# Block attention and an MLP on one core: inputs ahead of the layer-2 weights, and sixteen tiles transposed by the DMA crossbar

## The chip, the core and the metric

The kernel runs on one core of a Trainium2 chip. A core has five engines with instruction queues of their own: PE (matrix products and transposes, results in PSUM), DVE, ACT and POOL (elementwise work) and SP, which here only issues DMAs. The DMAs that SP issues form one hardware queue (q1 in the profile), those that POOL issues form another, software-driven one (q0). The metric is the device time in microseconds; the kernel before was timed three times, with a median of 247.38 us (247.32 to 247.84).

## What is computed

The inputs q, k and v have the shape (4, 8, 768, 64): batch, heads, positions, head dimension. The reference, cut to what matters:

```python
for b in range(nb):                                    # blocks of 64 positions
    intra = einsum(einsum(qb, kb) * Dmask, vb)         # decaying causal mask
    inter = einsum(qb * lam_pow, kv_state)
    out[:, :, sl] = intra + inter
    kv_state = lam_block * kv_state + einsum(kb * rev_pow, vb)
x  = out with the heads side by side                   # (4, 768, 512)
xn = (x - mean) / sqrt(var + 1e-06) * g_ln
y  = x + maximum(xn @ w_ch1, 0) @ w_ch2                # 512 -> 2048 -> 512
```

## The kernel before

**Tiles.** The 3072 rows (4 batches of 768) are 24 tiles of 128 rows, numbered t. Each tile passes through five steps, and then through the MLP in a group of one to four tiles.

- `p0(t)` (line 289) issues the loads of tile t+4 (`load_tile`, three DMAs of 256 KB on SP: kin, qin, vin) and turns tile t's inputs into bf16 on POOL (`bf_inputs`: kb line 142, qb line 144, vb line 146).
- `p1(t)` transposes kb and qb on PE (tk line 153, tq line 162); ACT copies tk to kTp and DVE copies tq to qT (ACT for the first four tiles).
- `p2(t)` multiplies kb by vb (pk, line 177), updates the state (Stmp on DVE line 184, Sn on POOL line 185), and makes the scores (sc, line 192), which DVE masks into mA (line 194).
- `p3(t)` makes the attention output po (lines 203 and 207), copies it to x on ACT (line 210) and lets DVE form the statistics and the centred, scaled bf16 tile xc (line 216).
- `p4(t)` transposes xc by four PE matmuls against an identity (xt, line 230), copies the result to the group's tile xT on ACT (line 231), and forms 1/std (lines 233 and 235).

`mlp(g)` gives two kinds of units. `m1(u)` multiplies xT by layer-1 weights (pm, line 254), with a ReLU on ACT into hT (line 257). `m2(i, part)` is four matmuls of hT by layer-2 weights (pm, line 267); after the fourth part DVE forms the output tile o (line 278) and SP stores it (line 280).

**Weights.** The weights are loaded by POOL in four chunks each, with a cast from float32 (w_0 to w_3 of layer 1 at line 75, of layer 2 at line 78). A chunk is 1 MB in HBM and 512 KB in the core's memory.

**Order.** All queues run in the order of the program text. Lines 309 to 353 are a hand-written start: four tiles of attention with the loading of weights between, the MLP of groups 0 and 1 (tiles 0 to 3), whose m2 units run chunk by chunk over three of the four tiles, and the attention of tiles 4 to 7 placed between MLP units by the table `after`. In it `load_tile(4, after_pool=True)` (line 319) puts a tiny memset into tile 4's input buffer on POOL, so that SP starts this load only when POOL has come there; tile 5 has the same at line 322. From line 356 on, a planner interleaves the steps of tiles 8 to 23 with the units of groups 4 to 9: after each unit it runs as many steps as a pace asks for, and all steps up to a group's last p4 within the last units before that group starts. The group sizes are 2, 2, 1, 1, 2, 3, 3, 4, 4, 2.

**Waits.** Each DMA of SP also waits for the DMA eight places earlier on that queue, since eight semaphores go round. The input buffers hold six tiles.

Of the kernel before, what the change touches and what calls it, by code (L numbers as in the profile page):

```python
# [8 lines left out]
BF16 = mybir.dt.bfloat16  # L9
# [7 lines left out]
def kernel(  # L17
# [30 lines left out]
    wk = ctx.enter_context(tc.tile_pool(name="wk", bufs=3))  # L48
    xp = ctx.enter_context(tc.tile_pool(name="xp", bufs=11))
    gp = ctx.enter_context(tc.tile_pool(name="gp", bufs=2))  # L50
    ps = ctx.enter_context(tc.tile_pool(name="ps", bufs=1, space=PSUM))


    qkv_in = {}

    def load_tile(t, after_pool=False):
        b, c = divmod(t, nb)
        got = {}
        for name, src in (("k", k), ("q", q), ("v", v)):
# [5 lines left out]
            nc.sync.dma_start(f, src[b, :, c * C:(c + 1) * C, :].rearrange("h p d -> p h d"))  # L65
            got[name] = f
        qkv_in[t] = got
# [6 lines left out]
    def load_w1(c):  # L74
        nc.gpsimd.dma_start(w1[c], moe_w_ch1[:, c * W1C:(c + 1) * W1C].rearrange("(k p) f -> p k f", p=128))
# [14 lines left out]
    ident = const.tile([128, 128], BF16)  # L90
# [19 lines left out]
    lamC = const.tile([128, NP, 128], F32)  # L110
# [17 lines left out]
    lam_cp = lam_c.rearrange("p (a two) -> p a two", two=2)  # L128
    nc.vector.tensor_copy(lamC[0:64, :, 0:64], lam_cp[0:64, :, 0:1].to_broadcast([64, NP, 64]))
    nc.vector.tensor_copy(lamC[64:128, :, 64:128], lam_cp[64:128, :, 1:2].to_broadcast([64, NP, 64]))  # L130


    st = {}
# [2 lines left out]
    mv_keep = {}  # L136
    xT_of = {}

    def bf_inputs(t):
        f = qkv_in.pop(t)  # L140
        kb = wk.tile([128, H, D], BF16, tag="kb", bufs=4, name="kb")
        nc.gpsimd.tensor_copy(kb, f["k"])  # L142
        qb = wk.tile([128, H, D], BF16, tag="qb", name="qb")
        nc.gpsimd.tensor_tensor(qb, f["q"], lam_q[:, :, None].to_broadcast([128, H, D]), op=ALU.mult)  # L144
        vb = wk.tile([128, H, D], BF16, tag="vb", bufs=4, name="vb")
        nc.gpsimd.tensor_tensor(vb, f["v"], lam_v[:, :, None].to_broadcast([128, H, D]), op=ALU.mult)  # L146
        st[t] = dict(qb=qb, kb=kb, vb=vb)

    def p1(t):
        s = st[t]  # L150
# [47 lines left out]
    def p3(t):  # L198
        s = st[t]
        po = ps.tile([128, H, D], F32, tag="po", bufs=1, name="po")  # L200
        inter = s["S"] is not None
        for h in range(H):
            nc.tensor.matmul(po[:, h, :], lhsT=s["mA"][:, h, :], rhs=s["vb"][:, h, :],  # L203
                             start=(h == 0), stop=(not inter and h == H - 1), skip_group_check=True)
        if inter:
            for p in range(NP):
                nc.tensor.matmul(po[:, 2 * p:2 * p + 2, :], lhsT=s["qT"][:, p, :], rhs=s["S"][:, p, :],  # L207
                                 start=False, stop=(p == NP - 1), skip_group_check=True)
        x = xp.tile([128, DM], F32, tag="x", name="x")
        nc.scalar.copy(x, po.rearrange("p h d -> p (h d)"))  # L210
        stats = wk.tile([128, 6], F32, tag="stats", name="stats")
        nc.vector.bn_stats(stats, x)  # L212
        mv = xp.tile([128, 2], F32, tag="mv", name="mv")
        nc.vector.bn_aggr(mv, stats)
        xc = wk.tile([128, DM], BF16, tag="xc", name="xc")
        nc.vector.scalar_tensor_tensor(xc, in0=x, scalar=mv[:, 0:1], in1=g_row, op0=ALU.subtract, op1=ALU.mult)  # L216
        s["xc"], s["mv"], s["x"] = xc, mv, x

    def p4(t):
        s = st.pop(t)  # L220
        g = group_of[t]
# [3 lines left out]
        if t < 2:  # L225
            xt = ps.tile([128, KA, 128], BF16, tag="mm", bufs=3, name="xt")
        else:
            xt = ps.tile([128, KA, 128], BF16, tag="aux", bufs=2, name="xt")
        for kk in range(KA):
            nc.tensor.transpose(xt[:, kk, :], s["xc"][:, kk * 128:(kk + 1) * 128], ident)  # L230
        nc.scalar.copy(xT_of[g][:, :, i * 128:(i + 1) * 128], xt)  # L231
# [49 lines left out]

        return m1, m2

    sizes = [2, 2, 1, 1, 2, 3, 3, 4, 4, 2]
    groups = [list(range(sum(sizes[:i]), sum(sizes[:i + 1]))) for i in range(len(sizes))]
    assert groups[-1][-1] == NT - 1
    group_of = {t: g for g, ts in enumerate(groups) for t in ts}

    def p0(t):
        if t > 3 and t + 4 < NT:  # L290
            load_tile(t + 4)
        bf_inputs(t)


    def p3_p0(t):
        p3(t)
        if t + 3 < NT:
            p0(t + 3)

    def round_of(j):  # L300
        steps = [(p1, j), (p3_p0, j - 1), (p2, j), (p4, j - 2)]
        return [(f, t) for f, t in steps if t < NT]

    def run(*steps):
        for f, *a in steps:
            f(*a)


    p0(0)
    p0(1)  # L310
    run((p1, 0), (p2, 0), (p0, 2), (p1, 1), (p3, 0), (p2, 1))
    load_w1(0)
    load_w1(1)
    run((p1, 2), (p3, 1))
    p0(3)
    load_w1(2)
    run((p2, 2), (p4, 0), (p1, 3), (p3, 2), (p2, 3), (p4, 1))
    load_w1(3)
    load_tile(4, after_pool=True)
    for c in range(NWC):  # L320
        load_w2(c)
    load_tile(5, after_pool=True)
# [5 lines left out]
    def m1s(f, c):  # L328
        for u in range(c * m1a.count // NWC, (c + 1) * m1a.count // NWC):
            f(u)  # L330

    m1s(m1a, 0)
    run((p3, 3), (p4, 2))
    m1s(m1a, 1)
    p4(3)
    m1s(m1a, 2)
    p0(4)
    for c in range(3):
        m1s(m1b, c)
    m1s(m1a, 3)  # L340
# [14 lines left out]

    steps = []
    for j in range(8, NT + 2):
        steps += [s for s in round_of(j) if s not in ((p3_p0, 7), (p4, 7), (p4, 6))]
# [12 lines left out]
    for u, (f, *a) in enumerate(plan):  # L371
        f(*a)

        rate = max([(upto(g) - pace) / max(1, at - 2 - u) for g, at in starts.items() if at > u] + [0.0])
        pace = min(len(steps), pace + rate)
        due = max([upto(g) for g, at in starts.items() if u < at <= u + 3] + [int(pace + 1e-6)])
        run(*steps[pos:due])
        pos = max(pos, due)
    run(*steps[pos:])
# [29 lines left out]
```

## Time and profile before

| | |
|---|---|
| median of three timed runs | 247.38 us |
| the profiled execution's own time | 246.76 us |
| its span, first to last instruction | 245.0 us |
| PE busy | 219.0 us (89%) |
| ACT, DVE, POOL busy | 121.1, 112.9, 92.9 us |
| HBM read, written | 27.53 MB, 6.29 MB |
| DMA, by queue | q1 25.43 MB in 78624 packets, q0 4.19 MB in 4224 packets |

Busy time is the union of an engine's instructions; the ends of matmuls are modelled and neighbours overlap, so that four short matmuls of 0.22 us each in the chain of work show 0.39 us in the timeline. In a timeline a row gives the start, the duration, the engine, the line, the operation, out<-in, the count, and in brackets the idle time of the engine before it with what ended it. The chain of work follows the work that ended last back from the end. The granted clock (PEclk) is the share of full speed that TensorE was given.

### The profile page before, as it was taken

What the parts mean: (1) busy time and instruction counts of PE and PEld (TensorE: products, weight loads), DVE (VectorE), ACT (ScalarE), POOL (GpSimd) and SP (SyncE); (2) the same over time, 40 slices, a digit from 0 to 9 for tenths busy, and PEclk for the clock granted to TensorE, in tenths of its full rate; (3) what the DMA queues carried; (4) which work ended last, traced back from release to release, by engine and by line L of the source; (5) the groups of instructions that cost most, each with busy time, mean ns of one, the idle gap of its engine ahead of it and who ended that gap; (6) DMA issues with size and microseconds to landing.
All of it is one profiled execution on the core that took longest, in us unless ns stands there. A gap on an engine that the chain in (4) does not pass through costs nothing.

```text
span 245.0 us, 4603 instructions
## 1 busy us (share of the span) xinstructions
PE 219.0 (89%) x1856; PEld 142.2 (58%) x1856; DVE 112.9 (46%) x217; ACT 121.1 (49%) x236; POOL 92.9 (38%) x107
## 2 busy tenths in 40 slices
PE   0676894499999897999999999999999999999993
PEld 0565683354587586767755676555555544444851
DVE  3366700033547656798547655475346531122111
ACT  5745775002175366657863487427862247611520
POOL 2779710159500866791566293063322000000000
PEclk9999999689999999999999999999999999999999
DMA  6999999999899999329951960111001120012102
GB/s 127 236 195 146 147 188 196 218 210 210 188 300 208 235 229 219 67 63 237 221 84 43 225 120 4 43 47 43 0 3 43 43 86 3 0 43 88 43 0 86
DMA packets 83012, 29.91 MB, mean 122 GB/s; under 512 B 75568, under 2 KB 79920, under 8 KB 82992
## 3 DMA queue, kind: packets, MB, share of 16 engines
q1 hardware_dynamic: 78624, 25.43, 48.0%
q0 software_dynamic: 4224, 4.19, 10.7%
q8 instruction: 14, 0.23, 0.4%
q14 instruction: 6, 0.05, 0.1%
q10 hardware_dynamic: 144, 0.00, 0.0%
HBM read 27.53 MB, written 6.29 MB: 138 GB/s over the span
## 4 chain that ended last, share of the span: by engine, by line
PE 76%; DMA 8%; ACT 6%; DVE 5%; POOL 2%; issue 2%; DVEq 0%; SPq 0%; ACTq 0%
PE pm L267 33%; PE pm L254 28%; DMA qin<-in_q_dram 7%; PE sc L192 4%; PE po L203 2%; PE xt L230 2%; PE tk L153 2%; PE tq L162 2%; PE po L207 2%; PE pk L177 1%; DVE stats L212 1%; DMA lam_b<-in_lam_dram 1%; ACT kTp L155 1%; ACT x L210 1%; ACT kTp L156 1%
## 5 line engine op out<-in xcount | busy, mean ns | idle before, releaser
L254 PE MATMUL pm<-xT,w 128*128 128x256 bf16 (+3 forms) x640 | 92.6, 298 | 0.7 <-ACT xT L231 0.7
L267 PE MATMUL pm<-w,hT 128*128 128x512 bf16 x384 | 90.5, 381 | 0.0
L257 ACT ACTIVATE hT<-pm 128x512 bf16<-128x512 f32 (+1 forms) x104 | 58.1, 564 | 41.2 <-PE pm L254 40.6
L254 PEld LDWEIGHTS <-w 128*128 128x128 bf16 x640 | 56.9, 99 | 23.8 <-issue 0.8
L267 PEld LDWEIGHTS <-hT 128*128 128x128 bf16 x384 | 36.1, 98 | 36.1 <-issue 0.6
L185 POOL TENSOR_TENSOR Sn<-Stmp,lamC 128x512 bf16<-128x512 f32 x16 | 20.4, 1273 | 69.0 <-DVE Stmp L184 69.0
L212 DVE BATCH_NORM_STATS2 stats<-x 128x6 f32<-128x512 f32 x24 | 16.7, 695 | 46.2 <-ACT x L210 46.1
L278 DVE SCALAR_TENSOR_TENSOR o<-pm,rstd,x 128x512 f32<-128x512 f32 (+1 forms) x25 | 18.0, 725 | 32.7 <-PE pm L267 32.5
L231 ACT COPY xT<-xt 128x512 bf16<-128x512 bf16 x24 | 14.0, 584 | 37.1 <-PE xt L230 37.0
L194 DVE TENSOR_TENSOR mA<-sc,tril 128x512 bf16<-128x512 f32 x48 | 30.7, 680 | 0.0
L144 POOL TENSOR_TENSOR qb<-qin,lam_q 128x512 bf16<-128x512 f32 x24 | 25.8, 1074 | 12.1 <-DMA qin<-in_q_dram 8.6
L146 POOL TENSOR_TENSOR vb<-vin,lam_v 128x512 bf16<-128x512 f32 x24 | 25.5, 1060 | 3.4 <-DMA vin<-in_v_dram 3.0
L155 ACT COPY kTp<-tk 64x512 bf16<-64x512 bf16 x24 | 13.7, 572 | 16.9 <-PE tk L153 16.8
L210 ACT COPY x<-po 128x512 f32<-128x512 f32 x24 | 14.1, 586 | 14.7 <-PE po L207 11.0
L142 POOL CAST kb<-kin 128x512 bf16<-128x512 f32 x24 | 16.6, 690 | 10.8 <-DMA kin<-in_k_dram 10.7
L216 DVE SCALAR_TENSOR_TENSOR xc<-x,mv,g_row 128x512 bf16<-128x512 f32 x24 | 20.2, 840 | 0.9
L162 PE MATMUL tq<-ident,qb 128*128 128x128 bf16 x96 | 10.4, 237 | 11.1 <-POOL qb L144 9.5
L167 DVE COPY qT<-tq 128x512 bf16<-128x512 bf16 x20 | 8.4, 419 | 21.5 <-PE tq L162 21.5
L153 PE MATMUL tk<-ident,kb 128*128 128x128 bf16 x96 | 10.2, 234 | 7.6 <-POOL kb L142 7.6
L192 PE MATMUL sc<-qT,kTp 128*128 128x128 bf16 x192 | 16.4, 234 | 0.3 <-ACT kTp L156 0.2
L192 PEld LDWEIGHTS <-kTp 128*128 128x128 bf16 x192 | 13.5, 106 | 1.3 <-ACT kTp L156 0.4
L156 ACT COPY kTp<-tk 64x512 bf16<-64x512 bf16 x24 | 13.9, 580 | 0.6
(43 smaller groups left out, 127.0 us busy)
## 6 DMA issues: line engine op xcount, KB each, us to landing
kin<-in_k_dram SPq DMA_DIRECT2D x24, 256.0 KB, 4.8
qin<-in_q_dram SPq DMA_DIRECT2D x24, 256.0 KB, 5.1
vin<-in_v_dram SPq DMA_DIRECT2D x24, 256.0 KB, 5.1
out_dram<-o SPq DMA_DIRECT2D x23, 256.0 KB, 2.2
w<-in_moe_w_ch_dram POOLq DMA_DIRECT2D x8, 512.0 KB, 8.7
g_row<-in_moe_g_ln_dram SPq DMA_DIRECT2D x1, 256.0 KB, 4.8
out_dram<-o SPq DMA_DIRECT2D x2, 128.0 KB, 1.7
lam_b<-in_lam_dram ACTq DMA_DIRECT2D x1, 4.0 KB, 3.0
```

The source lines that it names most:

```text
L142: nc.gpsimd.tensor_copy(kb, f["k"])
L144: nc.gpsimd.tensor_tensor(qb, f["q"], lam_q[:, :, None].to_broadcast([128, H, D]), op=ALU.mult)
L146: nc.gpsimd.tensor_tensor(vb, f["v"], lam_v[:, :, None].to_broadcast([128, H, D]), op=ALU.mult)
L185: nc.gpsimd.tensor_tensor(Sn, tmp, lamC, op=ALU.mult)
L192: nc.tensor.matmul(sc[:, i, :], lhsT=s["kT"][:, h // 2, h % 2, :], rhs=s["qT"][:, h // 2, :], start=(i == 0), stop=(i == H // 2 - 1), skip ...
L194: nc.vector.tensor_tensor(mA[:, half * (H // 2):(half + 1) * (H // 2), :], sc, tril[:, None, :].to_broadcast([128, H // 2, 128]), op=ALU.mult)
L212: nc.vector.bn_stats(stats, x)
L216: nc.vector.scalar_tensor_tensor(xc, in0=x, scalar=mv[:, 0:1], in1=g_row, op0=ALU.subtract, op1=ALU.mult)
L254: nc.tensor.matmul(pm[:, b, :], lhsT=w1[n // W2K][:, kk, (n % W2K) * 128:(n % W2K + 1) * 128], rhs=xT_of[g][:, kk, 0:N], start=(b == 0 and ...
L257: nc.scalar.activation(hT[:, u * NB:(u + 1) * NB, 0:N], pm, ACT.Relu)
L267: nc.tensor.matmul(acc[i], lhsT=hT[:, kk, i * 128:(i + 1) * 128], rhs=w2[kk // W2K][:, kk % W2K, :], start=(kk == 0), stop=(kk == KB - 1))
L278: nc.vector.scalar_tensor_tensor(o[:, sl], in0=a[:, sl], scalar=rstd, in1=x[:, sl], op0=ALU.mult, op1=ALU.add)
```

## The change

The diff, cut to its core:

```diff
-    def bf_inputs(t):
+    def in_k(t, eng):
+        kb = wk.tile([128, H, D], BF16, tag="kb", bufs=4, name="kb")
+        (eng.copy if eng is nc.scalar else eng.tensor_copy)(kb, qkv_in[t]["k"])
+        st[t] = dict(kb=kb)
+
+    def in_qv(t):
         f = qkv_in.pop(t)
-        kb = wk.tile([128, H, D], BF16, tag="kb", bufs=4, name="kb")
-        nc.gpsimd.tensor_copy(kb, f["k"])
...
-        xc = wk.tile([128, DM], BF16, tag="xc", name="xc")
+        xc = wk.tile([128, DM], BF16, tag="xc", bufs=4, name="xc")
...
+        dst = xT_of[g][:, :, i * 128:(i + 1) * 128]
+        if t >= 8:
+            nc.sync.dma_start_transpose(dst, s["xc"])
...
-    sizes = [2, 2, 1, 1, 2, 3, 3, 4, 4, 2]
+    sizes = [2, 2, 1, 1, 2, 2, 3, 4, 4, 3]
...
     def p0(t):
-        if t > 3 and t + 4 < NT:
-            load_tile(t + 4)
-        bf_inputs(t)
+        for n in {4: (), 5: (8, 9)}.get(t, (t + 4,)):
+            if n < NT:
+                load_tile(n)
+        in_k(t, nc.gpsimd)
+        in_qv(t)
...
-        steps = [(p1, j), (p3_p0, j - 1), (p2, j), (p4, j - 2)]
+        steps = [(p1, j), (p3_p0, j - 1), (p2, j)]
+        if j <= 11:
+            steps.append((p4, j - 1))
+        elif j > 12:
+            steps.append((p4, j - 2))
...
-    p0(0)
-    p0(1)
-    run((p1, 0), (p2, 0), (p0, 2), (p1, 1), (p3, 0), (p2, 1))
+    for t in range(2):
+        in_k(t, nc.vector)
+        in_qv(t)
...
+    run((p1, 0), (p2, 0), (p1, 1), (p3, 0))
+    in_k(2, nc.scalar)
+    in_qv(2)
     load_w1(0)
+    run((p2, 1), (p1, 2), (p3, 1))
+    in_k(3, nc.scalar)
+    in_qv(3)
     load_w1(1)
-    run((p1, 2), (p3, 1))
-    p0(3)
+    load_tile(4, after_pool=True)
+    run((p2, 2), (p4, 0), (p1, 3), (p3, 2))
     load_w1(2)
-    run((p2, 2), (p4, 0), (p1, 3), (p3, 2), (p2, 3), (p4, 1))
     load_w1(3)
-    load_tile(4, after_pool=True)
+    run((p2, 3), (p4, 1), (p0, 4))
     for c in range(NWC):
         load_w2(c)
     load_tile(5, after_pool=True)
...
-    p0(4)
     for c in range(3):
         m1s(m1b, c)
...
-        rate = max([(upto(g) - pace) / max(1, at - 2 - u) for g, at in starts.items() if at > u] + [0.0])
+        rate = max([(upto(g) - pace) / max(1, at - 6 - u) for g, at in starts.items() if at > u] + [0.0])
...
-        due = max([upto(g) for g, at in starts.items() if u < at <= u + 3] + [int(pace + 1e-6)])
+        due = max([upto(g) for g, at in starts.items() if u < at <= u + 7] + [int(pace + 1e-6)])
```

In words: tile 4 is loaded after the second chunk of layer-1 weights, and POOL converts it before it issues the layer-2 weights. The k inputs of tiles 0 and 1 are converted by DVE, those of 2 and 3 by ACT. The two copies that fill lamC move behind them on DVE. For tiles 8 to 23 the transpose of xc is a DMA that SP issues, straight into xT, and the PE matmuls and the ACT copy fall away. The planner has all of a group's p4 steps issued seven units before the group starts rather than three, tiles 8 to 10 get their p4 one round earlier, and the fifth and the last group have 2 and 3 tiles instead of 3 and 2.

On POOL, at the place where the loading of weights ends, this stands before (w_2 and w_3 with line 75 are layer 1; line 78 is layer 2; the memset at line 63 opens the load of tile 4, then that of tile 5; kb, qb and vb are tile 4's):

```order
L75 DMA w_2_77<-in_moe_w_ch_dram 128x4x512
L185 TENSOR_TENSOR Sn<-Stmp,lamC 128x512 x2
L75 DMA w_3_78<-in_moe_w_ch_dram 128x4x512
L63 MEMSET kin 128x1
L78 DMA w_0_79<-in_moe_w_ch_dram 128x4x512
L78 DMA w_1_80<-in_moe_w_ch_dram 128x4x512
L78 DMA w_2_81<-in_moe_w_ch_dram 128x4x512
L78 DMA w_3_82<-in_moe_w_ch_dram 128x4x512
L63 MEMSET kin 128x1
L142 CAST kb<-kin 128x512
L144 TENSOR_TENSOR qb<-qin,lam_q 128x512
L146 TENSOR_TENSOR vb<-vin,lam_v 128x512
```

And this stands there in the changed kernel, on the same engine:

```order
L75 DMA w_1_76<-in_moe_w_ch_dram 128x4x512
L63 MEMSET kin 128x1
L185 TENSOR_TENSOR Sn<-Stmp,lamC 128x512
L75 DMA w_2_77<-in_moe_w_ch_dram 128x4x512
L75 DMA w_3_78<-in_moe_w_ch_dram 128x4x512
L185 TENSOR_TENSOR Sn<-Stmp,lamC 128x512
L138 CAST kb<-kin 128x512
L144 TENSOR_TENSOR qb<-qin,lam_q 128x512
L146 TENSOR_TENSOR vb<-vin,lam_v 128x512
L78 DMA w_0_79<-in_moe_w_ch_dram 128x4x512
L78 DMA w_1_80<-in_moe_w_ch_dram 128x4x512
L78 DMA w_2_81<-in_moe_w_ch_dram 128x4x512
```

The memset that opens tile 4's load has moved ahead of the last two chunks of layer 1, and the four layer-2 issues now stand behind the three conversions of tile 4, each of which waits for a load.

On SP, where tiles 8 to 10 reach p4, only loads and stores stand before:

```order
L65 DMA kin<-in_k_dram 128x8x64
L65 DMA qin<-in_q_dram 128x8x64
L65 DMA vin<-in_v_dram 128x8x64
L280 DMA out_dram<-o 128x512
L65 DMA kin<-in_k_dram 128x8x64
```

In the changed kernel the transposes of tiles 8, 9 and 10 stand there on SP, between the loads of later tiles and the stores:

```order
L227 DMA_TRANSPOSE xT<-xc 128x4x128
L65 DMA kin<-in_k_dram 128x8x64
L65 DMA qin<-in_q_dram 128x8x64
L65 DMA vin<-in_v_dram 128x8x64
L227 DMA_TRANSPOSE xT<-xc 128x4x128
L284 DMA out_dram<-o 128x512
L65 DMA kin<-in_k_dram 128x8x64
L65 DMA qin<-in_q_dram 128x8x64
L65 DMA vin<-in_v_dram 128x8x64
L227 DMA_TRANSPOSE xT<-xc 128x4x128
```

Sixteen transposes have come into SP's queue; each waits for DVE's xc, and the loads and stores behind it wait with it.

More of the change, by code (lines that the diff above doesn't have):

```diff
@@ L127 @@
     nc.scalar.activation(sqrt_first, eps_t, ACT.Sqrt)
-    lam_cp = lam_c.rearrange("p (a two) -> p a two", two=2)
-    nc.vector.tensor_copy(lamC[0:64, :, 0:64], lam_cp[0:64, :, 0:1].to_broadcast([64, NP, 64]))
-    nc.vector.tensor_copy(lamC[64:128, :, 64:128], lam_cp[64:128, :, 1:2].to_broadcast([64, NP, 64]))
     st = {}
@@ L146, in bf_inputs @@
         nc.gpsimd.tensor_tensor(vb, f["v"], lam_v[:, :, None].to_broadcast([128, H, D]), op=ALU.mult)
[L147 removed]
+        st[t].update(qb=qb, vb=vb)
     def p1(t):
@@ L224, in p4 @@
             xT_of[g] = gp.tile([128, KA, GT * 128], BF16, tag="xT", bufs=3, name="xT")
-        if t < 2:
-            xt = ps.tile([128, KA, 128], BF16, tag="mm", bufs=3, name="xt")
-        else:
[L228 to L231, printed above, removed]
+        dst = xT_of[g][:, :, i * 128:(i + 1) * 128]
+        if t >= 8:
+            nc.sync.dma_start_transpose(dst, s["xc"])
+        else:
+            if t < 2:
+                xt = ps.tile([128, KA, 128], BF16, tag="mm", bufs=3, name="xt")
+            else:
+                xt = ps.tile([128, KA, 128], BF16, tag="aux", bufs=2, name="xt")
+            for kk in range(KA):
+                nc.tensor.transpose(xt[:, kk, :], s["xc"][:, kk * 128:(kk + 1) * 128], ident)
+            nc.scalar.copy(dst, xt)
         std = wk.tile([128, 1], F32, tag="std", name="std")
@@ L306, in run @@
             f(*a)
-    p0(0)
-    p0(1)
-    run((p1, 0), (p2, 0), (p0, 2), (p1, 1), (p3, 0), (p2, 1))
+    for t in range(2):
+        in_k(t, nc.vector)
+        in_qv(t)
+    lam_cp = lam_c.rearrange("p (a two) -> p a two", two=2)
+    nc.vector.tensor_copy(lamC[0:64, :, 0:64], lam_cp[0:64, :, 0:1].to_broadcast([64, NP, 64]))
+    nc.vector.tensor_copy(lamC[64:128, :, 64:128], lam_cp[64:128, :, 1:2].to_broadcast([64, NP, 64]))
+    run((p1, 0), (p2, 0), (p1, 1), (p3, 0))
+    in_k(2, nc.scalar)
+    in_qv(2)
     load_w1(0)
+    run((p2, 1), (p1, 2), (p3, 1))
+    in_k(3, nc.scalar)
+    in_qv(3)
     load_w1(1)
-    run((p1, 2), (p3, 1))
-    p0(3)
+    load_tile(4, after_pool=True)
+    run((p2, 2), (p4, 0), (p1, 3), (p3, 2))
     load_w1(2)
-    run((p2, 2), (p4, 0), (p1, 3), (p3, 2), (p2, 3), (p4, 1))
     load_w1(3)
-    load_tile(4, after_pool=True)
+    run((p2, 3), (p4, 1), (p0, 4))
     for c in range(NWC):
@@ L357 @@
     for j in range(8, NT + 2):
-        steps += [s for s in round_of(j) if s not in ((p3_p0, 7), (p4, 7), (p4, 6))]
+        steps += [s for s in round_of(j) if s not in ((p3_p0, 7), (p4, 7))]
     def upto(g):
```

## The prediction

> **What bounds the kernel now.** I read the page first: the busy times, the granted clock in 40 slices of 6.1 us, the DMA share, and the chain of work that ended last.
>
> ```profile
> PE 219.0 (89%) x1856; PEld 142.2 (58%) x1856; DVE 112.9 (46%) x217; ACT 121.1 (49%) x236; POOL 92.9 (38%) x107
> PEclk9999999689999999999999999999999999999999
> DMA  6999999999899999329951960111001120012102
> PE 76%; DMA 8%; ACT 6%; DVE 5%; POOL 2%; issue 2%; DVEq 0%; SPq 0%; ACTq 0%
> ```
>
> PE is busy for 89% of the span and holds 76% of the chain. What PE doesn't have to do is therefore saved, and what makes PE wait is lost. The clock dips in two slices only, the eighth and ninth, from 43 to 55 us. DMA is full in the first 16 slices, so the first 98 us can hide a wait for data. I then read PE's timeline where the clock dips, and a table of stretches around it (columns: stretch, length, busy time of PE, PEld, DVE, ACT, POOL with counts, granted clock, DMA share, GB/s).
>
> ```profile
> 27.87 1.91 PE L254 MATMUL pm<-xT,w 128*128 128x256 bf16 x16
> 30.45 8.90 PE L254 MATMUL pm<-xT,w 128*128 128x256 bf16 x80
> 39.19 0.39 PE L153 MATMUL tk<-ident,kb 128*128 128x128 bf16 x4
> 45.96 0.61 PE L162 MATMUL tq<-ident,qb 128*128 128x128 bf16 x4 [6.39 <-POOL qb L144]
> 46.37 3.62 PE L254 MATMUL pm<-xT,w 128*128 128x256 bf16 x16
> 49.78 1.80 PE L267 MATMUL pm<-w,hT 128*128 128x512 bf16 x4
> ...
> 40.00:46.00 6.00, 0.04 (x1) 0.04 (x2) 0.00 (x0) 1.02 (x2) 1.04 (x1) 0.88 1.22 196
> 46.00:52.00 6.00, 6.00 (x35) 3.99 (x36) 0.52 (x2) 1.19 (x2) 1.04 (x1) 0.56 1.07 217
> 76.00:96.00 20.00, 16.81 (x216) 13.84 (x214) 12.18 (x24) 12.53 (x24) 10.80 (x12) 1.00 1.09 227
> ```
>
> PE stands still for 6.39 us because tile 4's qb isn't there. Then it works at a granted clock of 0.56 for some 5 us: sixteen matmuls take 3.62 us, where the same sixteen took 1.91 us at 27.87. From 76 to 96 us PE idles 3.2 us of 20, in gaps so short that the clock stays at 1.00. Why qb is late stands in POOL's timeline, SP's timeline, and the landing times of the layer-2 weights (line 78):
>
> ```profile
> 28.17 2.97 POOL L78 DMA_DIRECT2D w<-in_moe_w_ch_dram  x4
> 37.56 0.61 POOL L142 CAST kb<-kin 128x512 bf16<-128x512 f32 x1 [6.31 <-DMA kin<-in_k_dram]
> 44.87 1.04 POOL L144 TENSOR_TENSOR qb<-qin,lam_q 128x512 bf16<-128x512 f32 x1 [6.70 <-DMA qin<-in_q_dram]
> 48.92 1.04 POOL L146 TENSOR_TENSOR vb<-vin,lam_v 128x512 bf16<-128x512 f32 x1 [3.02 <-DMA vin<-in_v_dram]
> ...
> 28.27 0.37 SPq L65 DMA_DIRECT2D kin<-in_k_dram  x1
> 48.66 1.06 SPq L65 DMA_DIRECT2D kin<-in_k_dram  x1
> 52.85 1.11 SPq L65 DMA_DIRECT2D qin<-in_q_dram  x1
> ...
> L78 POOL DMA_DIRECT2D w<-in_moe_w_ch_dram x4: 747/765/780, 28.2 to 30.4; - x4
> DMA to landing us min/median/max: 9.4/13.9/17.9
> ```
>
> Tile 4's three loads are issued at 28.3 us, a tenth of a microsecond after the first layer-2 chunk. While these chunks are under way an input of 256 KB takes 7.3 us (44.87 less 37.56); when they have landed, SP is let on to the next load every 1.05 us (the two rows at 48.66 and 52.85 are the first and the fifth of a run). The four chunks land from 37.6 (28.2 + 9.4) to 48.3 (30.4 + 17.9), 3.56 us apart. So the two queues share, and the inputs get the small part.
>
> **The change part by part.** The sum is made against the profiled execution, 246.76 us, which lies 0.62 us below the median of 247.38.
>
> *The stall.* The new order of POOL opens tile 4's load right after the second layer-1 chunk. To date it I need these rows of POOL, one layer-1 chunk that was issued alone at 27.33, and the rate of a stretch in which only layer-1 chunks moved:
>
> ```profile
> 16.57 1.26 POOL L185 TENSOR_TENSOR Sn<-Stmp,lamC 128x512 bf16<-128x512 f32 x1
> 27.33 0.80 POOL L75 DMA_DIRECT2D w<-in_moe_w_ch_dram  x1
> DMA to landing us min/median/max: 5.5/5.5/5.5
> 20.00:28.00 8.00, 6.20 (x70) 5.50 (x71) 5.46 (x12) 4.46 (x9) 6.50 (x7) 1.00 1.17 193
> ```
>
> POOL is through with tile 2's vb at 16.6 and goes on to Sn, as before, since these wait for loads whose order doesn't change. Then come one weight issue (0.8), Sn (1.26), tile 3's qb and vb (2 x 1.04), and the second weight issue at 20.8, tile 4's memset at 21.6. A chunk is 524 KB as it is written, at 193 GB/s 2.7 us; the one that landed 5.5 us after its issue began to flow after 2.8 us. So the second chunk flows from about 23.6. From there three chunks (3 x 2.7) and tile 4's three inputs (3 x 1.05) have to pass, in whatever order: 11.3 us, to 34.9. PE asks for tile 4's qb at 39.4. The stall of 6.39 us goes: **-6.39**. It is late only if these loads take over 4 us more than that.
>
> *The cold clock behind it.* The sixteen matmuls lose 1.71 us (3.62 less 1.91), tq 0.22 (0.61 less 0.39), the first four of m2 0.77 (1.80 against 1.03 for four at 81.21, below), together **-2.70**. The Trainium skill ("TensorE: Matmul & The Clock Gate", Part 1) says that the clock is halved after an idle window of about 3.4 us and given back after about 3.4 us of work; by that the loss would be some 1.7 us (an estimate) and the forecast 1.0 us higher. The trace has the low clock for longer here, so the sum goes by the trace.
>
> ```profile
> 81.21 1.03 PE L267 MATMUL pm<-w,hT 128*128 128x512 bf16 x4
> ```
>
> *What is late next: the layer-2 weights.* POOL now issues them behind tile 4's vb, which can start at 34.9 and takes 1.04. The first chunk flows 2.8 us after 36.0 and lands 2.7 later, at 41.5; the other three share with tile 5's loads and follow at 3.56 us, to 45.1, 48.6 and 52.2. PE, without the stall, has tk and tq of tile 4 and 16 matmuls behind 39.35 (0.44 + 1.8) and starts m2 at 41.6. A chunk serves three tiles (12 matmuls, 2.6 us), with 0.67, 0.45 and 0.22 us of attention between, so PE comes to the next three at 44.9, 47.9 and 50.7. The largest lateness is 1.5 us: **+1.5**. Its bounds are 0 (chunks at 2.7 us) and about 5 (each part of the start a microsecond later). No wait of this size lowers the clock by the row of 76 to 96 us.
>
> *The sixteen transposes.* In the chain of work each shows what it takes of PE's time. The matmuls of line 230 from 100 us on are 64, and the ACT copies are the page's:
>
> ```profile
> 103.30 0.86 PE pm L267 x4
> 104.16 0.22 PE xt L230 x4
> L230 PE MATMUL xt<-ident,xc x64: 219/219/219, 99.8 to 225.2; 128*128 128x128 bf16 x64
> L231 ACT COPY xT<-xt 128x512 bf16<-128x512 bf16 x24 | 14.0, 584 | 37.1 <-PE xt L230 37.0
> ```
>
> 64 matmuls are 16 tiles, 0.22 us each: **-3.52**, in full, as PE has no idle time there. ACT's sixteen copies of 0.58 us lie beside PE and bring nothing.
>
> *What the transposes as DMAs cost.* No row shows such a DMA. The nearest from this memory are the stores, the nearest in traffic the loads:
>
> ```profile
> out_dram<-o SPq DMA_DIRECT2D x2, 128.0 KB, 1.7
> out_dram<-o SPq DMA_DIRECT2D x23, 256.0 KB, 2.2
> kin<-in_k_dram SPq DMA_DIRECT2D x24, 256.0 KB, 4.8
> ```
>
> So 1.7 to 4.8 us to landing; I take 4, nearer the load, because the DMA digits of the page are high in some slices until 147 us. The room: the planner issues a group's last p4 seven units ahead. The tightest are tiles 20 and 23, which stand on SP behind the store of a tile whose m2 ended eight units (8 x 0.86 = 6.9 us) before the group starts; o and that store's issue take about 1.1, which leaves 5.8. Hidden: **0**, with cover of 1.8 us at each of five group starts. Behind a transpose that waits for xc, SP holds loads of tiles needed some four tiles later and stores that nobody waits for; the six input buffers cover that.
>
> *The planner.* It also sets p1 of tile 10 two units further behind p2 of tile 9. There PE now waits for DVE, since tq needs the PSUM buffer that Stmp frees:
>
> ```profile
> PE tq L162 <- DVE Stmp L184: 1.6, 1, 1.6
> ```
>
> Two units are 1.7 us, so it may go entirely; from 0 to -1.6, I take **-1.2**, as the other short gaps there stay.
>
> *At nothing.* The k casts of four tiles move from POOL (0.61 each, as at 37.56) to DVE and ACT. Until 16.6 us POOL waits for loads, and after that tile 2's scores wait for DVE, whose row of work is the same; between -0.4 and +0.5 us. Group sizes don't matter, because m1's time goes with the columns (256 and 512 here):
>
> ```profile
> 97.57 0.87 PE pm L254 x8
> 164.51 1.73 PE pm L254 x8
> ```
>
> *The sum.* -6.39 - 2.70 + 1.5 - 3.52 + 0 - 1.2 = -12.3. From 246.76 that is 234.45, and with the 0.62 to the median **235.1 us**.
>
> **The rivals.**
>
> *The layer-2 weights become the stall (0.15).* For it: POOL issues them 8 us later than before, behind a load, and PE's need and their landing lie within 1.5 us of each other. Against: DMA then carries less beside them, tile 4 being through. If the chunks come 5 us late in one wait, PE idles 5 instead of 1.5 us and works cold again, 2.7: 241.3 us. The skill's page on the clock puts that point at 3.4 us of idling.
>
> *The stall stays (0.05).* Tile 4's q crawls beside layer 1 as it did beside layer 2 and still misses 39.4 by six microseconds. The gain is then only the transposes and the planner: 247.38 - 4.7 = 242.7 us, as far as the change doesn't do what it says. Against it speaks that all three chunks and inputs together end at 34.9.
>
> *Transposes land late (0.08), the other side.* Each of five groups starts on a DMA instead of an ACT copy. Beyond 5.8 us from issue to landing PE waits at each start. The gain of 12.3 us is used up at 2.5 us per group, that is at 8.3 us; at 12 us PE loses 5 x 6.2 = 31 us and 2.7 of cold clock each time, less 12.3: about 280 us. For it: no row has this kind of DMA, it writes 256-byte rows, and input loads of 256-byte rows took 7.3 us when the queues were shared. The skill ("Advanced Engine Details and Errata", DMA Advanced Topics) lists the hardware path's transposes as less efficient than the software path's, though the same section calls them as fast as plain DMAs; nothing here shows either. Against: the weights are through by 52 us, and from 147 us on the DMA digits are 0 to 2.
>
> *SP's queue is blocked (0.04).* Transposes that wait for xc hold loads back until POOL lacks inputs, some 4 us: 239 us.
>
> **How the numbers follow.** The forecast has 0.68. Its own range is 232 (weights in time, -1.5; the gap gone, -0.4; 1.2 of the 3.2 us of short gaps) to 238.6 (weights at their bound, +3.5). The rivals that stay faster lie at 239 to 242.7; the range to **240.5** takes in the first part of them and leaves out the late transposes. Low end **231.8**. A measurement of this kernel can tell about 0.2% (0.5 us) from no change. Faster by more than that: 0.68 + 0.15 + 0.05 + 0.04 less a remainder of 0.01, that is 0.91; within it 0.01; slower 0.08.
>
> **What would show it.** Right: no dip of the granted clock between 43 and 55 us; tq of tile 4 straight behind the 80 matmuls; POOL's vb of tile 4 ending near 36 us; line 230's PE matmuls down to 32, with line 227's DMAs landing in under 5.8 us. Wrong: PE waits for layer-2 weights of over 3.4 us with a new dip, or waits of pm for xT at the five group starts after 100 us. Either shows among the longest waits.

## The result, and the profile after

The changed kernel takes 236.2 us (median of four runs, 235.61 to 236.77), beside 247.35 us (246.51 to 247.84) for the kernel before on the same chip: a ratio of 0.9552, with a 95% interval of 0.9517 to 0.9588. The profiled execution took 235.61 us with a span of 233.9 us, 11.15 us less than the 246.76 us of before. Of all the executions below, one is left out of every comparison: the profiled one of e10 took 584 us, with PE's matmuls of line 258 at 594 ns instead of 294.

Of the page of the changed kernel, the busy times, the granted clock and the DMA share:

```profile
PE 212.4 (91%) x1792; PEld 136.8 (58%) x1792; DVE 113.3 (48%) x219; ACT 114.3 (49%) x222; POOL 90.1 (39%) x103
PEclk9997799999999999999999999999999999999998
DMA  6998996999999999999999903310011200411012
```

PE has 64 instructions fewer and is busy for 6.6 us less: mostly the transposes (3.52) and the time that it worked at little over half speed (2.70). The dip of the clock at 43 to 55 us is gone; another stands in the fourth and fifth slice (17.5 to 29 us), which was not forecast. It is less new than the digits say. Before, four transposes of tile 3 took 0.61 us at 20.62, as long as tile 4's tq took in the low clock at 45.96, and yet the record of the clock reads 1.00 there:

```profile
20.62 0.61 PE L153 MATMUL tk<-ident,kb 128*128 128x128 bf16 x4 [1.53 <-POOL kb L142]
```

So a 9 in the clock's digits is no proof that PE ran at full speed: the durations of like matmuls have to be read beside it. Before, four of them took about 0.6 us up to 23.5 us. In the changed kernel they do so up to some 26 us, but for rows of 0.40 and 0.41 at 14.02, 15.66 and 20.03.

DMA is now nearly full through slice 23, to 134 us, where it had been so to 98.

PE's timeline of the changed kernel (start, duration, engine, line, tiles; in brackets what it waited for), at the start of layer 1, from its long stream on, and at the start of the group of tiles 8 and 9:

```profile
26.50 2.10 PE L258 MATMUL pm<-xT,w 128*128 128x256 bf16 x16 [0.67 <-ACT xT L235]
...
31.73 8.90 PE L258 MATMUL pm<-xT,w 128*128 128x256 bf16 x80
40.46 0.39 PE L153 MATMUL tk<-ident,kb 128*128 128x128 bf16 x4
40.69 0.39 PE L162 MATMUL tq<-ident,qb 128*128 128x128 bf16 x4
40.91 1.91 PE L258 MATMUL pm<-xT,w 128*128 128x256 bf16 x16
42.66 1.03 PE L271 MATMUL pm<-w,hT 128*128 128x512 bf16 x4
...
100.12 1.05 PE L258 MATMUL pm<-xT,w 128*128 128x256 bf16 x8 [0.85 <-DMA xT<-xc]
```

Tile 4's tq follows its tk without a pause, the sixteen matmuls behind it take 1.91 us instead of 3.62, and the first four of m2 take 1.03 instead of 1.80. Layer 1's long stream, though, starts 1.28 us later than before (31.73 against 30.45), and at 100 us PE waits for a transpose that a DMA does.

The table of stretches of the changed kernel (columns as in the prediction: length, busy time of PE, PEld, DVE, ACT, POOL, granted clock, DMA share, GB/s):

```profile
16.00:24.00 8.00, 4.44 (x51) 3.77 (x50) 5.87 (x8) 4.10 (x8) 7.60 (x9) 0.76 0.91 140
40.00:46.00 6.00, 6.00 (x55) 4.35 (x54) 2.31 (x4) 3.13 (x6) 1.21 (x1) 1.00 1.16 178
46.00:52.00 6.00, 5.94 (x41) 2.87 (x40) 1.79 (x4) 1.37 (x3) 0.67 (x2) 1.00 1.22 209
52.00:96.00 44.00, 42.44 (x478) 31.55 (x478) 27.01 (x51) 22.48 (x44) 27.98 (x29) 1.00 1.09 228
96.00:130.00 34.00, 32.75 (x328) 23.65 (x326) 24.45 (x49) 19.85 (x41) 20.48 (x23) 1.00 1.29 216
```

From 40 to 52 us, where the stall and the cold clock had been, PE idles 0.06 us. Its idle time now lies in 16 to 24 us (3.56 us; 2.01 before) and behind 52 us (1.56 and 1.25 us in the last two stretches). The DMA share of the last stretch is 1.29, where the same stretch of before had 0.71: the transposes and the loads pass there together.

POOL's timeline of the changed kernel at the start, the view of line 78 (the layer-2 weights) and that of line 227 (the transposes; the first row of each gives the time that an issue holds its engine, in ns, min/median/max, and the first and the last start):

```profile
17.70 1.29 POOL L185 TENSOR_TENSOR Sn<-Stmp,lamC 128x512 bf16<-128x512 f32 x1
18.93 1.05 POOL L144 TENSOR_TENSOR qb<-qin,lam_q 128x512 bf16<-128x512 f32 x1
19.93 1.04 POOL L146 TENSOR_TENSOR vb<-vin,lam_v 128x512 bf16<-128x512 f32 x1
...
21.71 0.12 POOL L63 MEMSET kin<- 128x1 f32 x1
...
34.96 1.04 POOL L146 TENSOR_TENSOR vb<-vin,lam_v 128x512 bf16<-128x512 f32 x1 [2.62 <-DMA vin<-in_v_dram]
```

```profile
L78 POOL DMA_DIRECT2D w<-in_moe_w_ch_dram x4: 750/766/812, 35.9 to 38.2; - x4
DMA to landing us min/median/max: 5.7/9.6/13.8
```

```profile
L227 SPq DMA_TRANSPOSE xT<-xc x16: 1191/1518/1924, 92.3 to 203.1; - x16
DMA to landing us min/median/max: 2.4/3.2/5.9
```

Tile 4's load opens at 21.71 (forecast 21.6) and its vb ends at 36.0 (forecast 36.0). The last layer-1 chunk landed at 34.5 us and tile 4's v at 34.9, where the sum had put the end of all these transfers. The layer-2 chunks land from 41.7 (35.95 + 5.7) to 52.0, as forecast, but PE comes 1 us later and hardly waits (0.06 us). The sixteen transposes take 2.4 to 5.9 us to land, and each holds SP for 1.2 to 1.9 us.

The longest of PE's waits that are new or changed:

```profile
PE po L203 <- DVE mA L194: 3.0, 3, 2.3
PE pm L258 <- DMA xT<-xc: 0.8, 1, 0.8
PE tq L162 <- DVE Sn L181: 0.4, 1, 0.4
```

The columns are the total, the number and the longest. The gap of 1.64 us at tile 10's tq is down to 0.40. One of the five group starts waits for a transpose. And PE waits at the start for tile 2's masked scores (mA), which it had not done. Why, DVE's timeline at 19 us shows, of before first (with what POOL does then) and of the changed kernel second:

```profile
17.78 1.68 POOL L75 DMA_DIRECT2D w<-in_moe_w_ch_dram  x2
18.98 1.12 DVE L216 SCALAR_TENSOR_TENSOR xc<-x,mv,g_row 128x512 bf16<-128x512 f32 x1
```

```profile
18.90 2.63 DVE L216 SCALAR_TENSOR_TENSOR xc<-x,mv,g_row 128x512 bf16<-128x512 f32 x1
```

The same operation, tile 1's xc, takes 2.63 instead of 1.12 us. Before, POOL was issuing weight chunks when it began. Now its end, 21.5 us, lies 0.56 us behind the end of POOL's run of Sn, qb and vb (20.97 us), and tile 2's mA comes behind it. The delay of layer 1 starts here and not in the clock: from the end of mA to layer 1's first matmul it is 3.3 us before and 3.2 us after.

### The profile page after: what moved, and what is told of

Same layout as the page of the kernel before. It is cut to its first block, busy times and chain, and to the rows that moved or that the text cites. A ratio compares the mean times of both kernels' runs of the same rounds, so it can differ in the third digit from the quotient of the medians.

```text
span 233.9 us, 4503 instructions
## 1 busy us (share of the span) xinstructions
PE 212.4 (91%) x1792; PEld 136.8 (58%) x1792; DVE 113.3 (48%) x219; ACT 114.3 (49%) x222; POOL 90.1 (39%) x103
## 4 chain that ended last, share of the span: by engine, by line
PE 70%; DMA 15%; SPq 4%; POOL 4%; DVE 3%; ACT 2%; issue 1%; DVEq 0%; ACTq 0%
PE pm L271 30%; PE pm L258 28%; DMA vin<-in_v_dram 7%; DMA w<-in_moe_w_ch_dram 6%; SPq L65 4%; PE sc L192 3%; PE po L203 2%; DMA xT<-xc 2%; PE tq L162 2%; PE po L207 1%; PE tk L153 1%; POOL vb L146 1%; PE pk L177 1%; DVE xc L216 1%; POOL w L78 1%
## 5 line engine op out<-in xcount | busy, mean ns | idle before, releaser
L258 PE MATMUL pm<-xT,w 128*128 128x256 bf16 (+3 forms) x640 | 90.4, 294 | 1.5 <-DMA xT<-xc 0.8
L271 PE MATMUL pm<-w,hT 128*128 128x512 bf16 x384 | 88.6, 379 | 0.1
L258 PEld LDWEIGHTS <-w 128*128 128x128 bf16 x640 | 56.2, 98 | 25.4 <-DMA xT<-xc 1.0
L216 DVE SCALAR_TENSOR_TENSOR xc<-x,mv,g_row 128x512 bf16<-128x512 f32 x24 | 20.7, 862 | 0.9
L138 POOL CAST kb<-kin 128x512 bf16<-128x512 f32 x20 | 13.2, 661 | 5.7 <-DMA kin<-in_k_dram 5.5
L162 PE MATMUL tq<-ident,qb 128*128 128x128 bf16 x96 | 9.7, 227 | 3.9 <-POOL qb L144 3.5
L203 PEld LDWEIGHTS <-mA 128*128 128x128 bf16 x192 | 9.0, 99 | 6.7 <-DVE mA L194 3.4
```

Of the source, the lines that this page charges most:

```text
L162: nc.tensor.transpose(tq[:, p, :], s["qb"][:, 2 * p:2 * p + 2, :], ident)
L258: nc.tensor.matmul(pm[:, b, :], lhsT=w1[n // W2K][:, kk, (n % W2K) * 128:(n % W2K + 1) * 128], rhs=xT_of[g][:, kk, 0:N], start=(b == 0 and ...
L271: nc.tensor.matmul(acc[i], lhsT=hT[:, kk, i * 128:(i + 1) * 128], rhs=w2[kk // W2K][:, kk % W2K, :], start=(kk == 0), stop=(kk == KB - 1))
```

## The experiments

All ratios are against the kernel before on the same chip. The start varies between the profiled executions: m2 begins at 42.7 us in the changed kernel and anywhere from 42.8 to 44.6 us in e1, e3, e4, e7 and e11, whose start is the same code. Much of this is PE's pace: layer 1's first sixteen matmuls take 1.91 us before, 2.10 in the changed kernel and up to 3.40 in these (e7, at a granted clock of 0.50). Each kernel has one profile, so times are compared by medians and ratios, single waits by the profiles, and a difference of medians under some 2 us may hold such a part.

**e1_start_only.** The new start with the old tail (xc keeps its fourth buffer):

```diff
-        if t >= 8:
+        if t >= NT:
-    sizes = [2, 2, 1, 1, 2, 2, 3, 4, 4, 3]
+    sizes = [2, 2, 1, 1, 2, 3, 3, 4, 4, 2]
...
+        steps = [(p1, j), (p3_p0, j - 1), (p2, j), (p4, j - 2)]
...
-        rate = max([(upto(g) - pace) / max(1, at - 6 - u) ...
+        rate = max([(upto(g) - pace) / max(1, at - 2 - u) ...
...
```

> The changed kernel with PE transposing every tile and with the old planner (group sizes, leads, p4 order as before): only the start differs from the kernel before. Theory (the start and the tail add up): the stall of 6.39 us and the cold clock of 2.7 us go, about 1.3 us of the start is lost, so some 7.5 us less than before, 239.5 to 240.5 us, with no dip of the clock at 43 to 55 us. Rival (the tail sets the end, through loads that come no sooner): PE waits later for inputs and most of the gain is given back, 243 us or more.

Measured: 240.14 us (239.14 to 241.01), ratio 0.9724 (0.9682 to 0.9765). Its longest wait behind 52 us is the old gap:

```profile
PE tq L162 <- DVE Stmp L184: 1.6, 1, 1.6
```

The start is worth 6.8 us of 246.94, and it leaves the gap at tile 10 as it was. The rival didn't come: PE waits for no inputs behind 52 us.

**e2_tail_only.** The old start with the DMA transposes, the new sizes, p4 places and leads, and xc's fourth buffer:

```diff
 before's kernel, and in p4:
+        if t >= 8:
+            nc.sync.dma_start_transpose(dst, s["xc"])
+        else:
...
 and sizes, round_of and the two leads as in the change
```

> The kernel before with the DMA transposes, the new group sizes, leads and p4 order, and the old start. Theory: 3.5 us of PE transposes and about 1.2 us of one gap go; the stall near 40 us stays; 242.5 to 243.5 us. Rival (the DMA transposes cost as much as they save, through a fuller DMA queue and SP issues of 1.2 to 1.9 us each): 246 to 248 us.

Measured: 243.25 us, ratio 0.9856 (0.9824 to 0.9887). The stall stands where it stood (6.4 us, the longest of the first row), and the gap of 1.64 us is down to 0.63:

```profile
PE tq L162 <- POOL qb L144: 9.2, 5, 6.4
PE tq L162 <- DVE Sn L181: 0.6, 1, 0.6
```

The two halves multiply to 0.9724 x 0.9856 = 0.9584, within the interval of the whole change (0.9517 to 0.9588): they add, 6.8 us and 3.6 us.

**e3_no_dma_tr.** The changed kernel with every transpose on PE:

```diff
-        if t >= 8:
+        if t >= NT:
```

> The changed kernel with PE transposing every tile, all else (start, planner, sizes) as changed. Theory: PE gets 16 x 0.22 us back to do and loses the one wait of 0.85 us for a landed transpose, so 2.7 us more than the changed kernel, 238.5 to 239.3 us. Rival (the planner and not the transposes brings the gain of the tail): within 0.7 us of the changed kernel's 236.2.

Measured: 241.31 us, ratio 0.9789 (0.9766 to 0.9812). That is 5 us above the changed kernel (5.9 by the two ratios), not the 2.7 that the theory had. PE's waits show where part of it lies (in all 1.3 us in the changed kernel):

```profile
PE xt L234 <- DVE xc L216: 3.6, 5, 1.3
```

Behind 52 us these waits are 2.2 us against 0.9 in the changed kernel. The new ones are at the transposes of tiles 8, 9 and 10, 0.40, 0.42 and 0.55 us, the tiles whose p4 the change puts one round closer to p3. A DMA queue may wait there for xc; PE, with its work in one order, waits itself. The longest, 1.33 us, is another matter: it stands at 33.4 us, in the start, where the same code waits 0.47 us in the changed kernel's execution.

**e10_pe_old_p4** follows this up: e3 with p4 back in its old place.

```diff
-        if j <= 11:
-            steps.append((p4, j - 1))
-        elif j > 12:
-            steps.append((p4, j - 2))
+        steps.append((p4, j - 2))
...
```

> The changed kernel with all transposes on PE (as in e3) and each tile's p4 back two rounds behind its p1, as before. e3 lost 5 us to the changed kernel where the 16 transposes are 3.5 us of PE. Theory: the rest of e3's loss is p4's place, with PE's transposes standing one round behind their xc and waiting for it (3.6 us in all in e3); with the old place these waits fall under 1.5 us and the time is 238.8 to 239.8. Rival: the rest of e3's loss came from its start alone, the waits move to another place, and the time stays at 240.8 to 241.5.

Measured: 240.3 us (median of five, 239.45 to 241.26), ratio 0.9739 (0.971 to 0.9767). Its profile is not usable (the 584 us above), so whether the waits went isn't shown. The result falls between theory and rival: p4's place accounts for 0.5% (1.2 us) of e3's loss by the two ratios, whose intervals just touch; the three new waits of e3 are 1.37 us. What is left over the changed kernel is 4.1 us by the times and 4.6 by the ratios, nearer to the 3.52 us of PE's transposes; the last microsecond is open.

**e4_short_lead.** The changed kernel with the planner's old lead, three units instead of seven:

```diff
-        rate = max([(upto(g) - pace) / max(1, at - 6 - u) ...
+        rate = max([(upto(g) - pace) / max(1, at - 2 - u) ...
-        due = max([upto(g) for g, at in starts.items() if u < at <= u + 7] + ...
+        due = max([upto(g) for g, at in starts.items() if u < at <= u + 3] + ...
```

> The changed kernel with the planner's lead put back from seven units to three. Theory (the seven units are the cover of the DMA transposes; 2.4 to 5.9 us from issue to landing do not fit in three units of 0.86 us): PE waits for xT at most of the five group starts, 1 to 2 us each, 238.5 to 244 us. Rival (the transposes need no such cover, since SP issues them early anyway): 236 to 237 us and at most one wait.

Measured: 243.75 us, ratio 0.9895 (0.9862 to 0.9928), 3.4% of the time back from the lead alone. All five group starts wait, and the longest wait is followed by 4 us at little over half the clock (PE's waits, its timeline, and the stretch behind the wait, below). Part of the difference in the profiles lies ahead of that: m2 begins at 44.6 us.

```profile
PE pm L258 <- DMA xT<-xc: 4.5, 5, 2.4
```

```profile
123.86 2.13 PE L258 MATMUL pm<-xT,w 128*128 128x384 bf16 x8 [2.45 <-DMA xT<-xc]
```

```profile
124.00:128.00 4.00, 4.00 (x25) 2.44 (x24) 0.51 (x1) 1.57 (x3) 0.00 (x0) 0.57 1.21 221
```

So the lead is what makes the transposes free: the work before each group start hides them, and with the old lead this cover is gone.

**e5_k_on_pool.** The changed kernel with the k casts of tiles 0 to 3 back on POOL, against the late xc:

```diff
-        in_k(t, nc.vector)
+        in_k(t, nc.gpsimd)
...
-    in_k(2, nc.scalar)
+    in_k(2, nc.gpsimd)
...
-    in_k(3, nc.scalar)
+    in_k(3, nc.gpsimd)
```

> The changed kernel with the k casts of tiles 0 to 3 back on POOL. In the changed kernel DVE's xc of tile 1 took 2.63 us instead of 1.12 while POOL went through Sn, qb and vb without a pause, and the layer-1 stream began 1.3 us later. Theory (POOL's unbroken run keeps DVE out of the memory that they share): the casts make POOL's run longer still, xc takes 2.6 us or more, and the time is 0.5 to 2 us above the changed kernel's 236.2. Rival (the casts on DVE and ACT hold those engines up): with them back on POOL the 1.3 us are regained, 234.5 to 235.5 us.

Measured: 236.04 us, ratio 0.9578 (0.9557 to 0.9598), no different from the changed kernel. The longer run of POOL makes xc longer, as the theory had it, but the time doesn't follow; theory and rival both miss on the time. The profile shows part of the reason: PE is 1.44 us later than in the changed kernel at 72 us, and then waits for tile 9's transpose 0.27 us instead of 0.85.

```profile
19.21 3.01 DVE L216 SCALAR_TENSOR_TENSOR xc<-x,mv,g_row 128x512 bf16<-128x512 f32 x1
```

**e6_w1_first.** The changed kernel with the issue of the second layer-1 chunk moved between POOL's Sn and tile 3's qb:

```diff
     in_k(3, nc.scalar)
-    in_qv(3)
     load_w1(1)
     load_tile(4, after_pool=True)
+    in_qv(3)
```

> The changed kernel with the second layer-1 chunk and tile 4's load opened ahead of tile 3's qb and vb on POOL, so that a weight issue of 0.8 us stands between Sn and qb. Theory (DVE's xc needs a pause of POOL): xc of tile 1 takes 0.8 to 1.2 us, the layer-1 stream begins about 1.3 us sooner, and tile 4 and the layer-2 weights come 1 to 2 us sooner: 234.3 to 235.3 us. Rival (xc is slow for another reason): xc stays near 2.6 us and the time at 236 to 236.7.

Measured: 236.03 us, ratio 0.9574 (0.9549 to 0.9599). The xc is short again and layer 1 begins at 24.97 instead of 26.50. But its first sixteen matmuls take 2.89 us instead of 2.10, so that m2 begins 0.72 us earlier (41.94), and the group of tiles 8 and 9 begins at the same time as in the changed kernel (100.12):

```profile
18.74 1.17 DVE L216 SCALAR_TENSOR_TENSOR xc<-x,mv,g_row 128x512 bf16<-128x512 f32 x1
```

```profile
PE pm L271 <- DMA w<-in_moe_w_ch_dram: 0.4, 1, 0.4
```

```profile
100.10 1.05 PE L258 MATMUL pm<-xT,w 128*128 128x256 bf16 x8 [1.20 <-DMA xT<-xc]
```

The 0.72 us end in two waits: 0.39 for the last layer-2 chunk at 51.6 us, where the changed kernel waits 0.06, and 0.35 more at 100 us, 1.20 instead of 0.85. So the second wait is set by when tile 9's transpose lands, not by PE. SP's queue of the changed kernel shows the reason:

```profile
92.28 1.49 SPq L227 DMA_TRANSPOSE xT<-xc  x1
93.86 0.52 SPq L65 DMA_DIRECT2D kin<-in_k_dram  x1
94.48 0.53 SPq L65 DMA_DIRECT2D qin<-in_q_dram  x1
95.10 0.87 SPq L65 DMA_DIRECT2D vin<-in_v_dram  x1
96.06 1.55 SPq L227 DMA_TRANSPOSE xT<-xc  x1
```

Tile 9's xc is ready at 92.6 us. Its transpose is issued at 96.06, behind tile 8's and behind the three loads of tile 16, and lands 4.0 us later. Four kernels test this.

**e7_from_10.** DMA transposes only from tile 10 on:

```diff
-        if t >= 8:
+        if t >= 10:
```

> The changed kernel with the DMA transposes from tile 10 on, tiles 8 and 9 by PE as before. Theory: the fifth group's wait of 0.85 us goes and PE does 0.44 us more, 0.4 us less than the changed kernel, 235.6 to 236.0 us. Rival (the wait only moves to the sixth group, whose transposes queue behind the same loads): 236.4 to 237.0 us.

Measured: 237.68 us, ratio 0.9638 (0.961 to 0.9666), 1.5 us slower, and so the theory failed. The wait for the DMA is gone, but PE does two more transposes (0.44 us) and waits for their xc, 0.40 and 0.42 us. These are 1.26 us against the 0.85 that went. The profile puts the rest into the start, which this edit doesn't touch: m2 begins 1.70 us later than in the changed kernel's execution, 1.30 of it in layer 1's first sixteen matmuls (3.40 us instead of 2.10). This execution took 237.69 us, about the median; whether the others start as late isn't shown. The exchange itself wins nothing: from tile 7's transpose (79.27) to tile 10's tq (107.01) PE needs 27.74 us, and 27.06 in the changed kernel.

**e8_both.** e6 and e7 together:

```diff
-        if t >= 8:
+        if t >= 10:
...
-    in_qv(3)
     load_w1(1)
     load_tile(4, after_pool=True)
+    in_qv(3)
```

> The two edits together: the second layer-1 chunk ahead of tile 3's qb and vb, and DMA transposes from tile 10 on. Theory: the gains add, 233.9 to 235.0 us, faster than both kernels. Rival (a PE that comes sooner waits for the layer-2 weights or for the loads instead): no faster than the better of the two alone.

Measured: 236.31 us, ratio 0.9598 (0.9574 to 0.9623): nothing over the changed kernel. The rival's wait is there: PE comes to layer 1's long stream early and waits 0.96 us for a layer-1 chunk, so that m2 begins at 42.58, hardly earlier than in the changed kernel (42.66):

```profile
PE pm L258 <- DMA w<-in_moe_w_ch_dram: 1.0, 1, 1.0
```

With the wait at 100 us in place the new order on POOL is worth nothing (0.9574 against 0.9552, intervals overlapping), without it 0.4% (0.9598 against 0.9638, overlapping from 0.961 to 0.9623). That would fit a gain which the wait at 100 us takes up, but isn't shown: e7's own start was 1.70 us late in its profile, which is more than the 0.4%.

**e9_load_behind.** e6 with the loads of tiles 16 and 17 behind the transposes of tiles 9 and 10:

```diff
             nc.sync.dma_start_transpose(dst, s["xc"])
+            if t in (9, 10):
+                load_tile(t + 7)
...
-        for n in {4: (), 5: (8, 9)}.get(t, (t + 4,)):
+        for n in {4: (), 5: (8, 9), 12: (), 13: ()}.get(t, (t + 4,)):
```

> The changed kernel with the second layer-1 chunk ahead of tile 3's q and v (as in e6), and with the loads of tiles 16 and 17 issued behind the transposes of tiles 9 and 10 instead of ahead of them. Theory: the start of the group of tiles 8 and 9 hangs on the order in SP's queue, since tile 9's xc is ready at 92.6 us and its transpose was issued only at 95.9, behind three loads. Then the transpose is issued near 93.6, lands before 98.5, the wait of 1.20 us at that start goes, and the time is 234.6 to 235.2, faster than the changed kernel. Rival: the DMA engines' backlog sets the landing (they are full up to 130 us), the transpose lands near 100 all the same, and the time stays at 235.8 to 236.3.

Measured: 235.05 us (234.57 to 236.45), ratio 0.9537 (0.9506 to 0.9568). SP's row of the transposes of tiles 8 and 9, and the group's start on PE:

```profile
92.73 2.76 SPq L227 DMA_TRANSPOSE xT<-xc  x2
```

```profile
99.43 1.04 PE L260 MATMUL pm<-xT,w 128*128 128x256 bf16 x8
```

Tile 9's transpose is issued at 94.29 and lands at 96.70, in 2.4 us instead of 4.0, and PE doesn't wait. The order in SP's queue made the wait: shown. The time is within the theory's range and the lowest of all, but its interval overlaps that of the changed kernel: it isn't shown to be faster than that one.

**e11_tr_on_act.** The transposes issued from ACT's queue:

```diff
-            nc.sync.dma_start_transpose(dst, s["xc"])
+            nc.scalar.dma_start_transpose(dst, s["xc"])
```

> The changed kernel with the sixteen transposes issued from ACT's queue instead of SP's. Theory: SP's long issues (1.2 to 1.9 us each) come from the descriptors of a transpose, not from SP; on ACT they hold up the copies and activations behind them, and ACT also stands still where it waits for xc, so that PE waits for ACT: 237 to 242, with the 0.85 us at the start of the group of tiles 8 and 9 gone or moved. Rival: the transposes were late only because SP had loads ahead of them; issued from ACT they land earlier, ACT's idle time covers the issue, and the time is 235 or less.

Measured: 237.86 us (235.97 to 238.54), ratio 0.9627 (0.9594 to 0.9661). ACT's timeline of this kernel, and PE's longest wait behind 52 us:

```profile
94.10 1.21 ACTq L227 DMA_TRANSPOSE xT<-xc  x1
95.36 0.29 ACT L237 ACTIVATE std<-mv,eps_t 128x1 f32<-128x1 f32 x1 [3.02 <-DVE mA L194]
```

```profile
PE tq L162 <- DVE Sn L181: 1.5, 1, 1.5
```

The issue holds ACT for 1.21 us as it held SP, and with the wait for tile 9's xc ahead of it ACT does no work for 3.02 us before tile 9's std. The wait at 100 us is gone, but the gap at tile 10's tq is back at 1.47 us. The time lies in the theory's range and is above the changed kernel's. But the profiled execution, 235.97 us, is the fastest of the six: the wait that went and the gap that came nearly cancel in it (0.85 against 1.07 us), and where the median's 1.7 us go isn't shown.

## Why the prediction was right

The forecast was 235.1 us, and 236.2 came out. Against the profiled execution, the terms:

| term | forecast, us | after, us | read from |
|---|---|---|---|
| stall at tile 4's qb | -6.39 | -6.39 | tq at 40.69, no wait |
| cold clock behind it | -2.70 | -2.70 | 1.91, 0.39 and 1.03 us |
| layer-2 weights late | +1.5 | +0.1 | 0.06 us idle from 46 to 52 |
| sixteen transposes | -3.52 | -3.52 | 64 matmuls fewer |
| transposes as DMAs | 0 | +0.85 | the wait at 100.12 |
| planner's gap | -1.2 | -1.24 | 1.64 to 0.40 |
| "at nothing": k casts, start | 0 | +1.28 | 31.73 against 30.45 |
| sum | -12.3 | -11.6 | profiled: -11.15 |

The remaining half microsecond is not traced to a cause.

- **The stall and the clock behind it** went by the mechanism that was forecast: the order in POOL's queue, with tile 4's load and vb dated within 0.1 us. e1 and e2 separate them: the new start alone brings 6.8 us where its three terms promised 7.6, and without it the stall is whole.
- **The layer-2 weights** landed where the sum put them. The step was mis-sized because PE came later: the forecast had m2 start at 41.6, and it started at 42.66. The late start of layer 1 and this term are two sides of one thing, and they nearly cancel; that the total came so close owes something to it. The margin is thin: in e1, e5 and e6 PE did wait for these chunks, 0.96, 0.47 and 0.39 us.
- **"At nothing"** was mis-sized by 1.28 us. The step said that "tile 2's scores wait for DVE, whose row of work is the same". The row was the same, but its length wasn't: with the k casts off POOL, Sn, qb and vb stand there without a pause, and DVE's xc, which reads two SBUF tiles beside them, took 2.63 us instead of 1.12. e6 puts a weight issue between and has 1.17 (1.28 and 1.67 in e8 and e9, with the same order), e5 makes the run longer and has 3.01, again ending 0.56 us behind the run. The Trainium skill ("SBUF — State Buffer", Who interferes with whom) says that only the port pair that DVE and GpSimd share causes contention, and that it is an exclusive lock; the three durations fit this. The trace doesn't show the lock itself.
- **The transposes as DMAs** were hidden at four of the five group starts, with a landing of 3.2 us in the middle (forecast 4, from 1.7 to 4.8) and 5.9 at most (forecast: late beyond 5.8). The step that failed is where the tightest start would be: the prediction looked at tiles 20 and 23 behind stores, which landed in 3.0 and 2.5 us, some 3 us before they were needed, and it came at tile 9, behind tile 8's transpose and tile 16's loads. Loads that "nobody waits for" hold the queue for a transpose that PE waits for. The rival of a blocked SP queue was right in its place, at a fifth of its price, and on the other side of the queue: not the loads were late, but the transpose. e4 shows what the rival of late transposes would have cost with less lead.
- **Terms in a row don't simply add.** In e6 m2 began 0.72 us earlier and the group at 100 us did not: the layer-2 weights took 0.39 of it and tile 9's transpose 0.35. Two delays, of which the later hangs on a queue and not on PE, cost the greater of the two there, not their sum.
- **"No wait of this size lowers the clock"** was said of 1.5 us, and stands for that: tq behind the gap of 1.64 us takes 0.38 us, in e1 and before. But e4's wait of 2.45 us did lower it, for 4 us at 0.57. The Trainium skill ("TensorE: Matmul & The Clock Gate", Part 1) puts the point at an idle window of about 3.4 us. This wait lies below it, so the run doesn't agree, and by the rule e4 would have lost only the wait.

## What to carry to other kernels

Moving a transpose from PE to a DMA brings PE's whole time only if it is issued early enough for its landing and nothing less urgent stands ahead of it in its queue; look for the tightest start among all groups by what is queued ahead, not only by the lead in units. When an engine's pauses are filled, look at who reads the same memory beside it. And before taking a wait away, ask whether the next one hangs on the same engine: if it hangs on a queue, the gain ends there.

## What the runs showed of the hardware

The first DMA queue of both kernels, of before first (packets, MB, share of 16 engines over the span):

```profile
q1 hardware_dynamic: 78624, 25.43, 48.0%
```

```profile
q1 hardware_dynamic: 87328, 27.53, 58.7%
```

Sixteen transposes are 8704 packets more, 544 each, of 241 bytes. The time of the queue's packets grows by 137.3 less 117.6, that is by 19.7 us of all sixteen engines. But this needn't all be the transposes' own. In e9, with the same packets, the growth is 11.9 us (55.5% of 233.4). In e11 the transposes have a queue of their own (q10; 144 of its packets are another load's):

```profile
q1 hardware_dynamic: 78624, 25.43, 52.7%
q10 hardware_dynamic: 8848, 2.10, 6.0%
```

There they take 6.0% of 234.3 us, 14.1 us or 0.88 us for each 128 KB. The loads and stores of q1, the same as before, take 123.5 us for 25.43 MB instead of 117.6, that is 1.27 us for 256 KB. So a byte that is transposed cost the engines 1.4 times as much of their time as a byte that is loaded or stored. The Trainium skill ("Advanced Engine Details and Errata", X-Bar Transpose) calls transposing DMAs as fast as regular ones; in this shape, from one on-chip tile of 128 x 512 to another, they took 1.4 times as long, though their landing was short enough to hide.

A transpose held the queue that issued it for 1.2 to 1.9 us on SP and 1.2 to 1.5 us on ACT, where the loads between two of them took SP 0.52 to 0.87 us (the five rows of SP above).
